# Batch 0's second product: block means copied at once, two masks on GpSimd, one pair's scores in a single excursion

## The chip, the cores and the metric

The kernel runs on one core of a Trainium2 chip. A core has a matrix engine (TensorE, PE in the profile), a vector engine (VectorE, DVE), an activation engine (ScalarE, ACT), a general engine (GpSimd, POOL) and a queue engine that issues transfers (SyncE, SP); transfers run on 16 DMA engines that all of these share. Each engine works through its own instructions strictly in the order in which the program lists them, and waits for the others at semaphores. The time is device microseconds for one execution, and the median over several executions is compared.

## The reference

Attention over 4 batches, 8 heads, 768 positions and head size 64, in which each position sees the 31 positions around it and 24 blocks of 32 positions in summary; then an MLP on the result.

```python
k_sum = k.reshape(B, H, nb, block, D).max(axis=3)      # block 32, nb 24
v_sum = v.reshape(B, H, nb, block, D).mean(axis=3)
scores_l = scale * np.matmul(q, k.transpose(0, 1, 3, 2))
mask_l = np.abs(pos[:, None] - pos[None, :]) < window  # window 16
scores_s = scale * np.einsum('bhsd,bhnd->bhsn', q, k_sum) + np.log(block)
scores_all = np.concatenate([np.where(mask_l, scores_l, -1e9), scores_s], axis=-1)
a = softmax(scores_all)
attn = np.matmul(a, np.concatenate([v, v_sum], axis=2))
x = attn.transpose(0, 2, 1, 3).reshape(B * S, H * D)   # 3072 x 512
h = x @ w_in                                           # 512 x 2048
out = (h * sigmoid(beta * h)) @ w_out                  # 2048 x 512
```

## The kernel before, in words

**Batches are staggered.** While the MLP of batch b runs on TensorE, the attention of batch b + 1 is woven into it. Each MLP has two products. The first (`h_half`, `h_tile`; lines 471 and 479) makes 16 tiles of h from xT, the transposed attention result. `h_tile` begins tiles 0 and 1 with twelve matmuls on xT of pairs 0 to 2 and only then takes pair 3's. The second makes 6 output tiles of 128 rows; each tile is 16 matmuls of 128x512 cut into 4 "atoms" of 4 matmuls (`o_atom`, matmul on line 497), so there are 24 atoms, numbered 0 to 23. The tiles alternate between two PSUM banks `one[0]` and `one[1]`; `o_out` copies a full tile to SBUF (on ScalarE for the first three tiles of batch 0, on VectorE otherwise) and SyncE stores it.

**Order by hand.** `run(main, sides)` lists the atoms; every side step carries a position, and a step with position p is issued behind atom floor(p), steps of one gap in the order of their positions. So a step at 8.99 comes behind atom 8 and one at 9.0 behind atom 9. The scheduler is manual: the order written is the order on each engine.

**Attention of batch 1 inside the second product of batch 0.** Heads go in 4 pairs g = 0 to 3, queries in two halves u = 0, 1.

- `scores(b, g, u, bg)` (matmuls on line 306) makes 24 score matmuls for both halves of a pair, 12 for each half, in the PSUM tile `big[2]` for u = 0 and `big[1]` for u = 1; `weigh` (line 315) takes the exponential on ScalarE into an SBUF tile `e` of 128x768; `mask_e` (line 319) multiplies that tile in place by the band mask on VectorE. In `scores` the mask follows at once for pairs 0 to 2. For pair 3 it follows inside `av`, behind the normalisation of pair 0.
- `vm_all` (line 368) makes the block means of all four pairs with 28 matmuls into `big[0]`, and four small copies, alternately on VectorE and ScalarE (`VMC`), take them to `vm_sb`.
- `spread(gg)` (line 379) copies the means of pairs 2gg and 2gg + 1 on VectorE into rows 96 to 127 of the two value tiles, two copies into `vo` and then two into `ve`. Before that, `v_odd_dma(g)` (lines 335 and 336) has moved shifted rows of `ve` to `vo` through SyncE's queue, reading those same rows of `ve`; the copies into `ve` wait for that transfer.
- `av_mm` (line 394) multiplies `e` by `ve` and `vo`, 24 matmuls for a pair, into `big[0]`, `big[1]`, `big[2]`, `big[0]` for pairs 0 to 3; `norm` (lines 420 and 421) divides by the sums on VectorE; `x_dma` (line 446) transposes the result into xT by a transfer that ScalarE's queue issues.
- `kq_cast` (line 455), on GpSimd, casts the keys of batch 2 as they arrive (`kst` to `kn`); the transfers that read `kn` are issued from SyncE (line 459) in the following stage.

Behind atom 8 lie `vm_all`, `spread(0)` and the scores of pair 2, half 0; behind atom 9 the scores of pair 2, half 1; behind atom 11 the scores of pair 3, `av` of pair 0 with the two masks of pair 3, and `spread(1)`; behind atom 14 `av` of pairs 1, 2 and 3.

Of the kernel before, what the change touches and what calls it, by code (L numbers as in the profile page):

```python
# [11 lines left out]
def kernel(  # L12
# [10 lines left out]
    nc = tc.nc  # L23
# [12 lines left out]
    QT = 64  # L36
# [5 lines left out]
    G = H // 2  # L42
# [224 lines left out]
    def km_pe(g, ks):  # L267
        key_max_win(g)
        key_sums(ks, g)
# [8 lines left out]
    def q_tile(g, h, m):  # L278
        return qn[g][h * D:(h + 1) * D, m * QT:(m + 1) * QT]
# [21 lines left out]
    def scores(b, g, u, bg):  # L301
        s = big[bg]
        for j in range(HT):
            m = u * HT + j
            for h in range(2):
                nc.tensor.matmul(s[:, h, j * QT:(j + 1) * QT], kw[g][h * D:(h + 1) * D, m, :], q_tile(g, h, m),  # L306
                                 start=True, stop=True)
        weigh(b, g, u, s)
        if g < G - 1:
            mask_e(b, g, u)  # L310

    def weigh(b, g, u, s):
        e = ep.tile([P, 2, HS], bf16, name="e", tag="e")
        et[(b, g, u)] = e
        return nc.scalar.activation(out=e[:], in_=s[:, :, 0:HS], func=ACTF.Exp, bias=bias[:, 0:1], scale=scale)  # L315

    def mask_e(b, g, u):
        e = et[(b, g, u)]
        nc.vector.tensor_mul(out=e.rearrange("p h (m q) -> p h m q", q=QT), in0=e.rearrange("p h (m q) -> p h m q", q=QT),  # L319
                             in1=mask[:, None, u * HT:(u + 1) * HT, :].to_broadcast([P, 2, HT, QT]))  # L320


# [11 lines left out]
    def v_odd_dma(g):  # L334
        nc.sync.dma_start(out=vo[0:QT, g, :, :], in_=ve[QT:P, g, :, :])
        nc.sync.dma_start(out=vo[QT:NK, g, 0:JV - 1, :], in_=ve[0:2 * W, g, 1:JV, :])
# [27 lines left out]
    def vm_all(t, cps):  # L364
        M = P - NK
        for j in range(J6 + 1):
            for g in range(G):
                nc.tensor.matmul(t[g * M:(g + 1) * M, 0, 0:2 * D], A[:, j],  # L368
                                 strided(ve[:, g, j, 0:1], [[J6 * VW, 2], [1, D]]),
                                 start=(j == 0), stop=(j == J6))  # L370
        for g in range(G):
            cps[g](vm_sb[NK:P, :, g], t[g * M:(g + 1) * M, 0, 0:2 * D].rearrange("p (h d) -> p h d", h=2))

    def spread(gg):
        r = slice(NK, P)
        s = slice(2 * gg, 2 * gg + 2)
        for tt in (vo, ve):
            for h in range(2):
                nc.vector.tensor_copy(out=tt[r, s, h * J6:(h + 1) * J6, 0:D],  # L379
                                      in_=vm_sb[r, h, s, None, :].to_broadcast([P - NK, 2, J6, D]))  # L380
# [5 lines left out]
    def av_mm(b, g, u, t):  # L386
        tv = t[:, 0:AVW].rearrange("p (j h e) -> p j h e", j=3, h=2)
        e = et[(b, g, u)]
        for j in range(3):
            J = 3 * u + j  # L390
            for h in range(2):
                for par in range(2):
                    lo = (2 * j + par) * QT
                    nc.tensor.matmul(tv[par * QT:(par + 1) * QT, j, h], e[:, h, lo:lo + QT],  # L394
                                     (vo if par else ve)[:, g, h * J6 + J, 0:D + 1], start=True, stop=True)
# [16 lines left out]
    def norm(b, g, t, us):  # L412
        t = t[:, 0:len(us)]
        n = len(us)
        if us[0] == 0:
            xn[(b, g)] = xp.tile([P, J6, 2, D], bf16, name="xn", tag="xn")
        x = xn[(b, g)]
        tv = t[:, :, 0:AVW].rearrange("p k (a e) -> p k a e", e=D + 1)
        r = xp.tile([P, n, 6], f32, name="r", tag="r")
        nc.vector.reciprocal(out=r[:], in_=tv[:, :, :, D])  # L420
        nc.vector.tensor_mul(out=x[:, 3 * us[0]:3 * us[0] + 3 * n].rearrange("p (k j) h d -> p k (j h) d", k=n),  # L421
                             in0=tv[:, :, :, 0:D], in1=r[:, :, :, None].to_broadcast([P, n, 6, D]))
# [188 lines left out]
    s = []  # L611
    wo = []

    def scale4(p, eng=None):
        for n in range(4 * p, 4 * p + 4):
            scale_w_out(n, eng)
# [18 lines left out]
    for g in (2, 3):  # L635
        s.append((g + .5, lambda g=g: mask_e(0, g, 1)))
# [6 lines left out]
    s = [(6, lambda: scale4(1)), (12, lambda: scale4(2)), (.5, clear_kw)]  # L643
# [11 lines left out]
    def scores_at(b, s, pos):  # L655
        for g in range(G):
            for u in range(2):
                s.append((pos[g] + .01 * u, lambda g=g, u=u: scores(b, g, u, (2, 1)[u])))
        s.append((pos[-1] + .02, silu_table))

    def av_at(b, s, pos, bufs):
        for g in range(G):
            def av(g=g):
                for u in range(2):
                    av_mm(b, g, u, big[bufs[g]][:, u])
                norm(b, g, big[bufs[g]], [0, 1])
                if g == 0:
                    for u in range(2):
                        mask_e(b, G - 1, u)
            s.append((pos[g], av))  # L670
# [9 lines left out]
    s = [(.05, exp_table), (.15, lambda: scale4(3)), (.7, lambda: km_pe(2, nc.gpsimd)), (2.9, lambda: km_pe(3, nc.gpsimd))]  # L680
    main = [lambda ms=ms, a=a: o_atom(0, ms, a) for ms in range(J6) for a in range(4)]
    for g in range(G):
        s.append(((2.5, 2.6, 2.7, 4.04)[g], lambda g=g: qt_pe(1, g, (0, 2, 1, 0)[g], dve_cp if g % 2 else act_cp)))
        s.append((3.3 + .1 * g, lambda g=g: v_cast(nc.gpsimd, g)))
        s.append((3.35 + .1 * g, lambda g=g: v_odd_dma(g)))
    scores_at(1, s, [4.05, 6.05, 8.99, 11.05])
    s.append((8.98, lambda: vm_all(big[0], VMC)))
    s.append((8.985, lambda: spread(0)))
    s.append((11.15, lambda: spread(1)))
    av_at(1, s, [11.1, 14.1, 14.2, 14.3], [0, 1, 2, 0])  # L690
    for g in range(G):
        s.append(((11.2, 14.35, 14.4, 14.5)[g], lambda g=g: x_dma(1, g)))
# [4 lines left out]
    for b in range(1, B):  # L697
        n = b + 1
        s = []
# [19 lines left out]
        s = [((x[0] - 16) * 1.2, x[1]) for x in late]  # L719
# [50 lines left out]
```

## Time and profile before

| | |
|---|---|
| median of 3 runs | 217.34 us (217.16, 217.34, 221.29) |
| profiled execution | 219.12 us |
| its span, first to last instruction | 217.4 us |
| around the span | 1.7 us |
| mean granted TensorE clock | 0.997 |
| TensorE busy | 206.3 us, 95% of the span |
| second product of batch 0 | 49.0 to 78.1 us |

Times in a view are microseconds from the first instruction. A row of a timeline has the start, the length, the engine, the line, the operation, what is written and read, and how many instructions are merged in it; in square brackets stands how long the engine was idle before it and what ended that idle time. The chain of waits follows the work that ended last back from the end: each piece was released by the one above it. In the view of one line or tile, three numbers with strokes are the shortest, the median and the longest instruction in ns.

### The profile page before, as it was taken

Reading aid. Unit: us, or ns where it says so; the run is one execution under the profiler, and the core shown is the slowest. Engines: PE = TensorE matmul, PEld = TensorE weight load, DVE = VectorE, ACT = ScalarE, POOL = GpSimd, SP = SyncE. Lnnn points to the kernel's source line nnn. Section 1 sums busy time; section 2 is a strip of 40 time slices with the busy share of each in tenths; the row PEclk is TensorE's granted clock in tenths of the full one; section 3 lists DMA queues with packets and bytes.
Section 4 is the critical chain, followed back from the end, with each engine's and each line's share of the span. In section 5 each row is a group of like instructions: output and inputs, shape, how many; then the busy total and the mean of one; then the engine's idle time right before and its main releaser. Section 6 shows DMA issues by size and latency. Waiting matters only on the chain.

```text
span 217.4 us, 5306 instructions
## 1 busy us (share of the span) xinstructions
PE 206.3 (95%) x2223; PEld 120.1 (55%) x2223; DVE 100.7 (46%) x235; ACT 107.6 (49%) x143; POOL 53.5 (25%) x88
## 2 busy tenths in 40 slices
PE   7779999999997999999999969999999999999993
PEld 7667666665454456664545436664555456654452
DVE  5576756697579611430799112521797200002121
ACT  2468586777773027667580037777570067750000
POOL 7928980010704200246103300246000000000000
PEclk9999999999999999999999999999999999999998
DMA  6999999999859939999669999999527410001212
GB/s 118 196 225 169 192 155 206 207 210 205 197 137 191 302 118 235 221 200 162 130 182 231 212 245 227 197 167 184 117 101 170 119 51 0 0 3 48 96 48 96
DMA packets 85271, 34.09 MB, mean 157 GB/s; under 512 B 73712, under 2 KB 82304, under 8 KB 85248
## 3 DMA queue, kind: packets, MB, share of 16 engines
q1 hardware_dynamic: 68192, 24.05, 54.5%
q0 software_dynamic: 7424, 7.34, 21.2%
q10 hardware_dynamic: 9632, 2.37, 7.2%
q8 instruction: 17, 0.28, 0.6%
q14 instruction: 6, 0.05, 0.1%
HBM read 27.37 MB, written 6.29 MB: 155 GB/s over the span
## 4 chain that ended last, share of the span: by engine, by line
PE 85%; DMA 7%; DVE 4%; issue 1%; POOL 1%; POOLq 0%; DVEq 0%
PE one L497 36%; PE big L479 28%; PE big L465 5%; DMA xT<-xn 4%; PE one L471 3%; DMA qrow<-in_q_dram 3%; PE big L306 3%; PE big L394 2%; PE big L255 2%; PE big L471 2%; DVE qn L242 1%; PE big L293 1%; PE big L285 1%; DVE xn L421 1%; PE big L368 1%
## 5 line engine op out<-in xcount | busy, mean ns | idle before, releaser
L497 PE MATMUL one<-w_out_sb,h_sb 128*128 128x512 bf16 (+1 forms) x400 | 86.5, 371 | 0.0
L492 ACT ACTIVATE h_sb<-big,beta_sb 128x768 bf16<-128x768 f32 x48 | 42.7, 900 | 55.5 <-PE big L479 55.5
L479 PE MATMUL big<-xT,w_in_sb 128*128 128x384 bf16 x384 | 63.1, 326 | 1.8 <-DMA xT<-xn 1.8
L497 PEld LDWEIGHTS <-h_sb 128*128 128x128 bf16 x400 | 37.7, 98 | 40.7 <-issue 0.2
L479 PEld LDWEIGHTS <-w_in_sb 128*128 128x128 bf16 x384 | 37.6, 98 | 27.1 <-issue 2.0
L242 DVE COPY o_sb<-one 128x512 f32<-128x512 f32 x20 | 13.8, 688 | 48.9 <-PE one L497 44.6
L315 ACT ACTIVATE e<-big,bias 128x768 bf16<-128x768 f32 x32 | 27.1, 898 | 7.9 <-PE big L306 4.9
L319 DVE TENSOR_TENSOR e<-e,mask 128x768 bf16<-128x768 bf16 x26 | 15.8, 631 | 18.0 <-ACT e L315 17.9
L236 POOL COPY kw<-km 128x288 bf16<-128x288 bf16 x12 | 5.2, 431 | 60.3 <-DVE km L232 38.7
L242 DVE COPY kw<-kT 128x1152 bf16<-128x1152 bf16 x8 | 3.8, 474 | 24.0 <-DMA kT<-kn 24.0
L324 POOL CAST ve<-vst 128x832 bf16<-128x832 f32 x15 | 13.3, 909 | 4.9 <-DMA vst<-in_v_dram 3.1
L455 POOL CAST kn<-kst 128x768 bf16<-128x768 f32 x8 | 6.9, 867 | 26.6 <-DMA kst<-in_k_dram 26.6
L421 DVE TENSOR_TENSOR xn<-big,r 128x768 bf16<-128x768 f32 (+1 forms) x14 | 12.6, 900 | 0.5
L232 DVE TENSOR_REDUCE km<-kT 128x24 bf16<-128x768 bf16 x12 | 11.2, 944 | 2.3 <-ACT kT L239 2.3
L465 PE MATMUL big<-xT,w_in_sb 128*128 128x384 bf16 x64 | 11.4, 326 | 0.0
L609 ACT ACTIVATE h_sb<-big,beta_sb 128x384 bf16<-128x384 f32 x16 | 8.1, 579 | 2.7 <-PE big L465 2.7
L471 PEld LDWEIGHTS <-w_in_sb 128*128 128x128 bf16 x64 | 6.1, 98 | 4.0
L394 PEld LDWEIGHTS <-e 128*64 128x64 bf16 x336 | 6.3, 111 | 3.4 <-issue 3.1
L471 PE MATMUL one<-xT,w_in_sb 128*128 128x384 bf16 x44 | 8.1, 326 | 0.0
L465 PEld LDWEIGHTS <-w_in_sb 128*128 128x128 bf16 x64 | 5.9, 98 | 3.5
L306 PEld LDWEIGHTS <-kw 64*128 64x128 bf16 x288 | 4.9, 95 | 4.8 <-issue 3.0
L394 PE MATMUL big<-ve,e 128*64 128x65 bf16 x150 | 6.4, 196 | 1.3 <-DVE ve L379 1.3
(121 smaller groups left out, 184.0 us busy)
## 6 DMA issues: line engine op xcount, KB each, us to landing
out_dram<-o_sb SPq DMA_DIRECT2D x23, 256.0 KB, 2.5
vst<-in_v_dram SPq DMA_DIRECT2D x13, 336.0 KB, 4.7
kst<-in_k_dram SPq DMA_DIRECT2D x8, 384.0 KB, 5.9
qst<-in_q_dram SPq DMA_DIRECT2D x8, 384.0 KB, 4.3
w_in_sb<-in_moe_w_in_dram POOLq DMA_DIRECT2D x4, 512.0 KB, 6.1
w_out_sb<-in_moe_w_out_dram POOLq DMA_DIRECT2D x4, 512.0 KB, 13.7
vo<-ve SPq DMA_DIRECT2D x12, 107.2 KB, 2.3
vst<-in_v_dram SPq DMA_DIRECT2D x3, 416.0 KB, 6.7
```

The source lines that it names most:

```text
L242: nc.vector.tensor_copy(out=o, in_=i)
L306: nc.tensor.matmul(s[:, h, j * QT:(j + 1) * QT], kw[g][h * D:(h + 1) * D, m, :], q_tile(g, h, m), start=True, stop=True)
L315: return nc.scalar.activation(out=e[:], in_=s[:, :, 0:HS], func=ACTF.Exp, bias=bias[:, 0:1], scale=scale)
L319: nc.vector.tensor_mul(out=e.rearrange("p h (m q) -> p h m q", q=QT), in0=e.rearrange("p h (m q) -> p h m q", q=QT), in1=mask[:, None, u * ...
L324: eng.tensor_copy(out=ve[:, g, lo:hi, 0:D], in_=vst[g][:, lo:hi])
L394: nc.tensor.matmul(tv[par * QT:(par + 1) * QT, j, h], e[:, h, lo:lo + QT], (vo if par else ve)[:, g, h * J6 + J, 0:D + 1], start=True, sto ...
L421: nc.vector.tensor_mul(out=x[:, 3 * us[0]:3 * us[0] + 3 * n].rearrange("p (k j) h d -> p k (j h) d", k=n), in0=tv[:, :, :, 0:D], in1=r[:, ...
L465: nc.tensor.matmul(t[:, 0:HS], w_in_sb[:, ki, i * P:(i + 1) * P], xT[:, ki, 0:HS], start=(ki == 0), stop=(ki == k1 - 1))
L471: nc.tensor.matmul(t[:, 0:HS], w_in_sb[:, ki, i * P:(i + 1) * P], xT[:, ki, lo:lo + HS], start=(ki == 0), stop=(ki == k1 - 1))
L479: nc.tensor.matmul(t[:, kk, 0:HS], w_in_sb[:, ki, i * P:(i + 1) * P], xT[:, ki, kk * HS:(kk + 1) * HS], start=(ki == 0), stop=(ki == k1 - 1))
L492: nc.scalar.activation(out=h_sb[:, i, :].rearrange("p (k m) -> p k m", k=2), in_=t[:, :, 0:HS], func=ACTF.Silu, scale=beta_sb[:, i:i + 1])
L497: nc.tensor.matmul(t[:, 0:hi - lo], h_sb[:, n, ms * P:(ms + 1) * P], w_out_sb[:, n, lo:hi], start=(n == 0), stop=(n == k2 - 1))
```

## The change

Four edits, all for batch 1's attention inside the second product of batch 0. The later batches keep their order and their engines.

1. `spread(1)` moves from behind atom 11 (position 11.15) to behind atom 8 (8.982), right behind `spread(0)` and ahead of pair 2's scores.
2. The two masks of pair 3 are issued in `scores`, right behind the exponentials, and on GpSimd instead of VectorE; `av` of pair 0 issues them no longer.
3. Pair 2's scores move from 8.99 and 9.00 to 8.985 and 8.995, so that both halves come behind atom 8 with no atom between them.
4. `spread(0)` moves from 8.985 to 8.981, which keeps it ahead of pair 2's scores.

```diff
@@ scores(b, g, u, bg)
         weigh(b, g, u, s)
-        if g < G - 1:
+        if g < G - 1 or b == 1:
             mask_e(b, g, u)
@@ mask_e(b, g, u)
-        nc.vector.tensor_mul(out=e.rearrange(
+        (nc.gpsimd if (b, g) == (1, G - 1) else nc.vector).tensor_mul(out=e.rearrange(
...
@@ av_at(b, s, pos, bufs)
                 norm(b, g, big[bufs[g]], [0, 1])
-                if g == 0:
+                if g == 0 and b > 1:
                     for u in range(2):
                         mask_e(b, G - 1, u)
@@ second product of batch 0
-    scores_at(1, s, [4.05, 6.05, 8.99, 11.05])
+    scores_at(1, s, [4.05, 6.05, 8.985, 11.05])
     s.append((8.98, lambda: vm_all(big[0], VMC)))
-    s.append((8.985, lambda: spread(0)))
-    s.append((11.15, lambda: spread(1)))
+    s.append((8.981, lambda: spread(0)))
+    s.append((8.982, lambda: spread(1)))
     av_at(1, s, [11.1, 14.1, 14.2, 14.3], [0, 1, 2, 0])
```

The resulting order on the engines: on VectorE, the four copies of `spread(1)` now follow those of `spread(0)`, then the two masks of pair 2, then the four normalisations. On GpSimd, the two masks of pair 3 stand between the last cast of values (line 324) and the first cast of batch 2's keys (line 455). ScalarE and SyncE keep their order.

More of the change, by code (lines that the diff above doesn't have):

```diff
@@ L318, in mask_e @@
         e = et[(b, g, u)]
-        nc.vector.tensor_mul(out=e.rearrange("p h (m q) -> p h m q", q=QT), in0=e.rearrange("p h (m q) -> p h m q", q=QT),
+        (nc.gpsimd if (b, g) == (1, G - 1) else nc.vector).tensor_mul(out=e.rearrange("p h (m q) -> p h m q", q=QT), in0=e.rearrange("p h (m q) -> p h m q", q=QT),
                              in1=mask[:, None, u * HT:(u + 1) * HT, :].to_broadcast([P, 2, HT, QT]))
```

## The prediction

> **What bounds the kernel now.** I read the page first, then the chain of waits in order of time, then the timeline of each engine over the second product of batch 0.
>
> ```profile
> span 217.4 us, 5306 instructions
> PE 206.3 (95%) x2223; PEld 120.1 (55%) x2223; DVE 100.7 (46%) x235; ACT 107.6 (49%) x143; POOL 53.5 (25%) x88
> ```
>
> TensorE is busy 95% of the span, so a change elsewhere pays only where TensorE stands still or spends time on switching. The chain of waits (start, length, what) shows this stage and, from 111 us, the same stage of the next batch:
>
> ```profile
> 60.29 0.28 PE big L306 x12
> 60.58 0.97 PE one L497 x4
> 61.55 0.28 PE big L306 x12
> 61.83 1.83 PE one L497 x8
> 63.66 0.46 PE big L306 x24
> 64.12 0.55 PE big L394 x24
> ...
> 66.29 1.18 DVE e L319
> ...
> 67.48 0.63 DVE vo L379 x2
> 68.11 1.18 DVE ve L379 x2
> 69.29 0.04 issue
> 69.33 0.92 PE big L394 x44
> 70.25 7.88 PE one L497 x36
> 78.13 20.80 PE big L479 x128
> ...
> 111.58 2.70 PE one L497 x12
> 114.27 1.26 PE big L394 x72
> ...
> 120.01 7.98 DMA xT<-xn
> ```
>
> Between 64 and 69 us the chain leaves TensorE: normalisation, masks of pair 3 and the copies of `spread(1)` run on VectorE, and the last two of those copies release the product with the values. TensorE's own timeline shows the hole:
>
> ```profile
> 64.55 2.76 PE L497 MATMUL one<-w_out_sb,h_sb 128*128 128x512 bf16 x12
> 67.24 0.22 PE L394 MATMUL big<-ve,e 128*64 128x65 bf16 x1
> 69.06 0.19 PE L394 MATMUL big<-ve,e 128*64 128x65 bf16 x1 [1.25 <-DVE ve L379]
> 70.19 7.94 PE L497 MATMUL one<-w_out_sb,h_sb 128*128 128x512 bf16 x36
> ```
>
> Pairs 1 to 3 take from 67.24 to 70.19, 2.95 us. In the next batch the same 72 matmuls take 1.26. So 1.69 us are lost here, and no removal of this wait can give more.
>
> **Pair 2 in one excursion.** Two visits of 12 score matmuls, with 4 and then 8 output matmuls, take 0.28 + 0.97 + 0.28 + 1.83 = 3.36 us (60.29 to 63.66). In one visit 24 score matmuls take 0.46 (63.66) and the 12 output matmuls behind them 2.70 (111.58): 3.16. Gain 0.2, so everything behind it on TensorE comes 0.2 earlier: pair 3's scores at 63.46, atoms 12 to 14 ending at 67.04 instead of 67.24. The second half needs `big[1]`, which the exponential of pair 1 left long before, and ScalarE's order does not change:
>
> ```profile
> 61.56 1.69 ACT L315 ACTIVATE e<-big,bias 128x768 bf16<-128x768 f32 x2
> 63.70 0.58 ACT L239 COPY o_sb<-one 128x512 f32<-128x512 f32 x1 [0.45 <-PE one L497]
> 64.18 1.70 ACT L315 ACTIVATE e<-big,bias 128x768 bf16<-128x768 f32 x2
> ```
>
> **The block means earlier.** VectorE gets four copies ahead of pair 2's masks:
>
> ```profile
> 61.82 0.62 DVE L379 COPY ve<-vm_sb 32x768 bf16<-32x768 bf16 x2
> 62.49 0.56 DVE L319 TENSOR_TENSOR e<-e,mask 128x768 bf16<-128x768 bf16 x1
> ...
> L335 SPq DMA_DIRECT2D vo<-ve x1: 483/483/483, 61.0 to 61.0; - x1
> DMA to landing us min/median/max: 2.2/2.2/2.2
> ```
>
> `spread(0)` ends at 62.44. The two `vo` copies of `spread(1)` take 0.63 (row 67.48) to 63.07. The two `ve` copies must wait for pair 3's shift transfer, issued at 61.0 and landed 2.2 later, at 63.2; so this wait costs 0.15, and queued behind it are pair 2's masks and the normalisation of pair 0. The copies end at 63.85. Pair 2's exponentials end at 62.4 and 63.25 (row 61.56), so its masks, 0.54 apart, run to 64.95, and the normalisation of pair 0 (0.23 + 0.96) ends at about 66.15, where it ended at 65.91. Who waits for these: pair 2's product at 67.04 + 0.42 = 67.46 for the masks, 2.5 us of slack; pair 3's product at 67.88 for `big[0]`, which the normalisation empties, 1.7 us of slack; and pair 0's transposing transfer, 0.2 us later. Nothing on TensorE's path. That is the first edit's price: nothing, with these slacks as cover.
>
> **The masks on GpSimd.** This is what is late next. The exponentials of pair 3 start 0.2 earlier with the atom that precedes them, at 63.98, and end at 64.83 and 65.68. GpSimd has been idle since its last value cast, so it starts about 64.88. TensorE wants half 0 of pair 3 at 67.88 and half 1 at 68.09. Two masks of t each release half 1 at 64.88 + 2t; with 0.05 for the signal (0.04 in the row at 69.29) and 0.21 for the last 12 matmuls, TensorE leaves at 65.14 + 2t, but not before 67.04 + 1.26 = 68.30.
>
> No GpSimd instruction with two tensor inputs is in the trace, so t is bounded by neighbours:
>
> ```profile
> 66.03 1.03 POOL L455 CAST kn<-kst 128x768 bf16<-128x768 f32 x1 [6.66 <-DMA kst<-in_k_dram]
> 67.85 0.95 POOL L455 CAST kn<-kst 128x768 bf16<-128x768 f32 x1 [0.79 <-DMA kst<-in_k_dram]
> 70.36 0.83 POOL L455 CAST kn<-kst 128x768 bf16<-128x768 f32 x1 [1.56 <-DMA kst<-in_k_dram]
> L319 DVE TENSOR_TENSOR e<-e,mask x2: 547/790/1033, 58.8 to 59.7; 128x768 bf16<-128x768 bf16 x2
> L319 DVE TENSOR_TENSOR e<-e,mask x2: 548/862/1177, 65.8 to 66.3; 128x768 bf16<-128x768 bf16 x2
> ```
>
> One input of 768 elements costs 0.83 undisturbed (70.36) and 1.03 beside VectorE (66.03). Below: t = 0.83, if the second input is free. Above: 2 x 1.03 = 2.06, if the inputs are read one behind the other and disturbed. I take 2 x 0.83 = 1.66, since a cast already moves an element in about the time that reading one takes, and VectorE has little of the disturbing kind left there. With it TensorE leaves at 68.46 instead of 70.19: 1.73 gained, of 1.89 (0.2 + 1.69) at most; at 2.06, 69.26 and 0.93. The Trainium skill, "GPSIMD Engine Reference", section 4.1 "Engine selection", speaks against the edit: it gives elementwise products to VectorE, and section 3.1 has 4497 ns for 2048 elements of a two-input add. An estimate by that figure is 1.69 us for 768, and the sum would be 0.06 less; no run so far shows the operation.
>
> The second cost is a collision. Alone a mask on VectorE takes 0.55; the one begun at 66.29 took 1.18 and ended at 67.47, 0.41 behind the cast that had begun at 66.03 and ended at 67.06. So it stood until GpSimd was done. Pair 2's second mask starts at 64.4, GpSimd at 64.88: VectorE is first, and GpSimd may start 0.1 late, which I charge. If it is the other way round, the mask stands until 64.88 + 1.66 = 66.54, ends at 66.95, and the normalisation of pair 0 at 68.15, 0.27 behind TensorE's need of `big[0]`: TensorE leaves at 68.15 + 0.05 + 0.42 = 68.62, 0.16 worse. The Trainium skill, "SBUF — State Buffer", says of the port pair that the two engines share that it is "an exclusive lock, not a bandwidth split"; the 1.18 against 0.55 agrees.
>
> Behind the masks on GpSimd stand the key casts: the first moves from 66.03 to about 68.3. Their readers are transfers issued at 81.48:
>
> ```profile
> 81.48 2.54 SPq L459 DMA_TRANSPOSE kT<-kn  x1
> ```
>
> That is cover of some 10 us. Moving the masks off VectorE also removes two instructions (64.95 to 67.47 in the chain is mostly theirs), so the normalisations of pairs 1 to 3 run at 67.5, 68.7 and 69.8 without a queue.
>
> **What is late after that.** TensorE reaches the next product 1.63 earlier, at 76.5, and wants xT of pairs 0 to 2 there, and of pair 3 twelve matmuls on (20.80/128 x 12 = 1.95), at 78.45.
>
> ```profile
> L446 ACTq DMA_TRANSPOSE xT<-xn x2: 1252/1274/1296, 71.9 to 73.3; - x2
> DMA to landing us min/median/max: 3.6/3.6/3.6
> DMA to landing us min/median/max: 3.6/4.0/7.3
> ```
>
> Before, pairs 2 and 3 were issued at 71.9 and 73.3 and landed 3.6 later, at 75.5 and 76.9, against needs at 78.13 and 80.08. After, they are issued at about 70.0 and 71.3 and land by 73.6 to 75.6. The slack stays above 2 us.
>
> **Sum.** 0.2 from the single excursion, 1.69 from the hole, less 0.16 for half 1 of pair 3 and 0.1 for the collision: 1.63 us. The profiled execution, 219.12 with its span of 217.4, would lose that from its span: 215.8. The median of the runs, 217.34, is below that execution; the same 1.63 off it gives 215.7.
>
> **Rivals.**
>
> *GpSimd is slower than two reads.* Break-even is 65.14 + 2t = 70.19, t = 2.5 us. At four times the single read, 3.3 us, TensorE leaves at 71.74, 1.55 later than before: 218.9. For it: GpSimd has no such row here. Against: its one-input rows lie at 0.83 to 1.03. Chance 0.17, from 217.3 upward.
>
> *A first-use price on GpSimd.* If the first product there has to fetch its code, the whole stage waits. Against it: the first copy of its kind is as quick as the rest.
>
> ```profile
> 8.79 0.52 POOL L331 COPY vo<-ve 64x384 bf16<-64x384 bf16 x1
> 18.48 0.50 POOL L331 COPY vo<-ve 64x384 bf16<-64x384 bf16 x1
> ```
>
> It loses from 1.63 us up, and 2% from 4.35 + 1.63 = 6 us up; priced at that edge, 217.34 + 4.35 = 221.7. The same page of the Trainium skill, section 2.1, puts a first call into a freshly loaded kernel library at about 6 us; nothing here shows such a load. Chance 0.05.
>
> *The gain meets a late transfer.* With 7.3 us to landing, as the slowest had it (beside the key loads), instead of 3.6, pair 2's transfer would land at 70.0 + 7.3 = 77.3, 0.8 behind the need: 216.5. Chance 0.12. Further on, the next stage ends in a transfer of 7.98 us (120.01) that TensorE waits for. If that end were fixed by transfers that do not move with TensorE, all would be lost: 217.3. Against: the loads of that stage stand on SyncE's queue behind the output stores, which move along. Chance 0.06.
>
> **How the numbers follow.** Forecast 215.7 with 0.60, its own range 215.3 to 216.4 (t from 0.83 to 2.06, and 0.1 to 0.2 of spread between runs). The range to 217.9 takes in both transfer cases and the near edge of the slow mask: 0.8 of the chance; its low end, 215.2, is 217.34 less 1.89 less 0.2. About 2%, 4.35 us here, is what a measurement of this kernel can tell from no change. The holes are too small for a gain of 4.35; a loss of that size needs the first-use price or masks of 4.7 us each: 0.06.
>
> **What would show it.** In the profile after: a single visit of 24 score matmuls near 60.3; `spread(1)` ending near 63.9; two rows of GpSimd on line 319 of about 1.66 us each, the first near 64.9; pairs 1 to 3 on TensorE in about 1.4 us from 67.0, with at most a wait of 0.2 on GpSimd; the next product starting near 76.5 without a wait on xT. Rows of GpSimd over 2.5 us, or a wait on xT at 76.5, make it wrong.

## The result and the profile after

| | before | changed |
|---|---|---|
| median of 20 runs each | 218.32 us (216.97 to 221.29) | 217.12 us (215.01 to 220.72) |
| ratio | | 0.994, 95% interval 0.9915 to 0.9966 |
| profiled execution, its span | 219.12, 217.4 us | 219.29, 217.6 us |

The change is faster by 0.6%: 1.3 us by the ratio, 0.7 to 1.9 by its interval. The ratio counts only executions within 1.5% of the fastest of the same kernel; the medians count all. The forecast was 215.7 us, which is 1.6 us under the 217.34 us of the three runs that were known, but 2.6 us under the 218.32 us that the same kernel has over 20 runs.

The page of the changed kernel, with the row of the granted TensorE clock in 40 slices of 5.4 us:

```profile
span 217.6 us, 5307 instructions
PEclk9958999999999999999999999999999999999999
```

The profiled execution had a low clock from about 11 to 22 us, long ahead of the change, so the two spans cannot be set against each other, and I compare stages: from the first output matmul (line 497) to the first matmul of the next product (line 479). Over all sets of runs, the executions that the ratio counts and whose mean granted clock was 0.997 or more have means of 217.6 us before (51 runs) and 216.6 changed (20 runs), 1.0 us apart.

The chain of waits of the changed kernel through the stage (start, length, what):

```profile
62.28 0.51 PE big L368 x28
62.79 0.46 PE big L306 x24
63.24 2.71 PE one L497 x12
...
65.98 0.49 ACT o_sb L239
66.46 0.91 ACT e L315
...
67.45 3.25 POOL e L319 x2
...
70.75 0.38 PE big L394 x12
71.13 7.88 PE one L497 x36
79.00 20.80 PE big L479 x128
```

One visit of 24 score matmuls, then 12 output matmuls, as drawn up. The chain now leaves TensorE for ScalarE's exponential and GpSimd's two masks instead of VectorE's queue. The timelines of VectorE and GpSimd beside it:

```profile
65.41 0.62 DVE L379 COPY ve<-vm_sb 32x768 bf16<-32x768 bf16 x2
66.06 1.03 DVE L319 TENSOR_TENSOR e<-e,mask 128x768 bf16<-128x768 bf16 x2
67.45 3.24 POOL L319 TENSOR_TENSOR e<-e,mask 128x768 bf16<-128x768 bf16 x2 [6.04 <-ACT e L315]
70.64 1.60 POOL L455 CAST kn<-kst 128x768 bf16<-128x768 f32 x2
```

The masks of pair 2 are over at 67.09, before GpSimd starts; GpSimd's two take 3.24, 1.64 each by the instruction; the key casts wait behind them and nobody waits for those.

The lengths of the parts in us, read from the starts of these matmuls in every profile. "Hole" is the time that TensorE stood still behind another engine ahead of the products with the values (line 394), from its timeline. "Over 20.80" is what the next first product took over its 20.80 us, mostly the wait on xT near 125 us.

| profile | ahead of the stage | hole | stage | over 20.80 |
|---|---|---|---|---|
| before | 49.0 | 1.25 | 28.95 | 1.97 |
| before, c1 | 49.2 | 1.19 | 28.88 | 3.89 |
| before, d1 | 50.6 | 1.30 | 28.99 | 0.48 |
| before, d2 | 48.6 | 0.53 | 28.22 | 0.00 |
| n1, before without key loads | 52.0 | 1.25 | 28.94 | 0.00 |
| n3, the same again | 48.9 | 1.23 | 28.92 | 0.00 |
| changed | 51.5 | under 0.1 | 27.32 | 1.27 |
| changed, c0 | 49.5 | under 0.1 | 27.32 | 0.35 |
| changed, d1 | 49.1 | under 0.1 | 27.32 | 1.29 |
| changed, d2 | 49.0 | under 0.1 | 27.32 | 1.57 |
| n2, changed without key loads | 49.0 | under 0.1 | 27.31 | 0.00 |
| e1, masks on VectorE | 49.5 | under 0.1 | 27.12 | 0.42 |
| e8, the same again | 48.9 | under 0.1 | 27.26 | 0.76 |
| e2, means early only | 49.0 | under 0.1 | 27.26 | 1.39 |
| e3, one excursion only | 48.9 | 1.19 | 28.67 | 0.67 |
| e4, masks on GpSimd only | 51.4 | 1.88 and 0.68 | 31.77 | 0.41 |
| e5, second mask twice | 49.2 | 1.78 | 29.03 | 0.48 |
| e6, changed, later key loads | 49.1 | under 0.1 | 27.33 | 0.31 |
| e7, e1 with later key loads | 49.2 | under 0.1 | 27.05 | 1.73 |
| e9, keys late in the kernel before | 51.0 | under 0.1 | 27.69 | 1.36 |

The stage went from 28.95 to 27.32, 1.63 us: the forecast's sum to the hundredth. It is the same in all four profiles of the changed kernel. What is not the same is the stage of the kernel before (28.22 in one of its profiles) and the wait on xT at the end of the next stage, which both kernels have. It was the first of these rows of waits in the first profile of the kernel before, and the second in that of the changed kernel:

```profile
PE big L479 <- DMA xT<-xn: 1.8, 1, 1.8
...
PE big L479 <- DMA xT<-xn: 1.1, 1, 1.1
```

### The profile page after: what moved, and what is told of

It is laid out like the page before. It is cut to its first block, busy times and chain, and to the rows that moved or that the text cites. A ratio compares the mean times of both kernels' runs of the same rounds, so it can differ in the third digit from the quotient of the medians.

```text
span 217.6 us, 5307 instructions
## 1 busy us (share of the span) xinstructions
PE 208.4 (96%) x2223; PEld 122.1 (56%) x2223; DVE 99.1 (46%) x233; ACT 107.8 (50%) x143; POOL 56.9 (26%) x90
## 4 chain that ended last, share of the span: by engine, by line
PE 85%; DMA 7%; POOL 3%; DVE 2%; issue 1%; ACT 1%; POOLq 0%; DVEq 0%
PE one L497 35%; PE big L479 28%; PE big L465 5%; DMA xT<-xn 4%; PE one L471 3%; DMA qrow<-in_q_dram 3%; PE big L255 2%; PE big L306 2%; PE big L394 2%; PE big L471 2%; POOL e L319 1%; PE big L293 1%; PE big L368 1%; POOL krow L85 1%; PE big L285 1%
## 5 line engine op out<-in xcount | busy, mean ns | idle before, releaser
L319 DVE TENSOR_TENSOR e<-e,mask 128x768 bf16<-128x768 bf16 x24 | 13.7, 592 | 18.2 <-ACT e L315 18.0
L473 ACT ACTIVATE h_sb<-one,beta_sb 128x384 bf16<-128x384 f32 x11 | 6.4, 582 | 1.5 <-PE one L471 1.0
```

Of the source, the lines that this page charges most:

```text
L319: (nc.gpsimd if (b, g) == (1, G - 1) else nc.vector).tensor_mul(out=e.rearrange("p h (m q) -> p h m q", q=QT), in0=e.rearrange("p h (m q) ...
```

## The experiments

**The changed kernel again, and the edits one by one.** c0, e1, e2 and e3 were run against the same runs of the kernel before.

c0 is the changed kernel itself:

> The changed kernel once more, as the control of this set. Theory (the stage gives 1.63 us and keeps it): about 1.6 us under the kernel before run beside it, ratio 0.9925. Rival (some of the gain is met by the transposing transfer that TensorE waits for at the end of the next stage): the stage is still 1.6 us shorter, but the ratio lies at 0.995 to 0.998 and the wait on xT near 128 us is longer than in the kernel before.

Ratio 0.9962, interval 0.993 to 0.9994: 0.1 to 1.5 us, again less than the stage's 1.63. The ratio lies where the rival put it, but not for the rival's reason: the wait at the end of the next stage was shorter here (0.35 against 1.97), not longer.

e1 keeps the masks of pair 3 on VectorE (shown against the changed kernel):

```diff
-        if g < G - 1 or b == 1:
+        if g < G - 1:
...
-        (nc.gpsimd if (b, g) == (1, G - 1) else nc.vector).tensor_mul(
+        nc.vector.tensor_mul(
...
-                if g == 0 and b > 1:
+                if g == 0:
```

> All of the change but the GpSimd edit: the two masks of pair 3 stay on VectorE behind the normalisation of pair 0. Theory (the hole came from the late copies of the block means, and GpSimd's 1.62 us masks leave a wait of 0.2 to 0.3 us): the masks end by 68.0 on the clock of the kernel before, TensorE does not wait, the stage is 1.8 to 1.9 us shorter than before and 0.2 shorter than in the changed kernel; ratio 0.991 to 0.992. Rival (VectorE's queue was the trouble, so the masks must leave it): the masks, which also meet the key casts on GpSimd, end after 68.6, TensorE waits for them by 0.5 us or more, and the kernel is slower than the changed one.

Ratio 0.9871 (0.9813 to 0.9928, six runs); e8, the same kernel again:

> The variant with the masks of pair 3 on VectorE once more, since its first set had few runs. By its stage (1.83 us shorter than before, with no wait left in it) 216.0 to 216.2 where the kernel before has 217.9, ratio 0.991 to 0.993. The 0.987 of its first set would need 2.8 us, more than the stage lost; if it comes again, something behind the stage has gained too.

Ratio 0.9936 (0.9903 to 0.9968), 1.4 us, where its stage is 1.69 shorter; the 0.987 did not come again. In e1 VectorE's masks run beside a key cast, as the timelines of GpSimd and VectorE show:

```profile
66.82 1.20 POOL L455 CAST kn<-kst 128x768 bf16<-128x768 f32 x1 [7.48 <-DMA kst<-in_k_dram]
66.78 1.64 DVE L319 TENSOR_TENSOR e<-e,mask 128x768 bf16<-128x768 bf16 x2
```

They take 1.64 instead of 1.03, and still the chain of waits has TensorE do its 72 matmuls in 1.33, against 1.26 undisturbed:

```profile
67.53 1.33 PE big L394 x72
```

So the GpSimd edit was not needed. Without it the stage is 0.06 to 0.20 shorter. That lead over the changed kernel is too small for the timing to settle.

e2 moves only `spread(1)` (and `spread(0)` to stay ahead of it) in the kernel before:

```diff
-    s.append((8.985, lambda: spread(0)))
-    s.append((11.15, lambda: spread(1)))
+    s.append((8.981, lambda: spread(0)))
+    s.append((8.982, lambda: spread(1)))
```

> Only the copies of the block means of pairs 2 and 3 move ahead; masks on VectorE as before, pair 2's scores in two visits. Theory: it alone removes the hole, 1.6 to 1.7 us, ratio 0.992. Rival (each edit gives a share): under 1 us.

Stage 27.26, so this one edit alone shortens it by 1.69, as much as the whole change does; ratio 0.9929 (0.9887 to 0.9972). Its chain shows pairs 1 to 3 without a stop:

```profile
67.29 1.26 PE big L394 x72
```

e3 moves only pair 2's scores (and `spread(0)` to stay ahead of them) in the kernel before:

```diff
-    scores_at(1, s, [4.05, 6.05, 8.99, 11.05])
+    scores_at(1, s, [4.05, 6.05, 8.985, 11.05])
...
-    s.append((8.985, lambda: spread(0)))
+    s.append((8.981, lambda: spread(0)))
```

> Only pair 2's scores are put into one visit. Theory: 0.2 us less between the first scores of pair 2 and the scores of pair 3 (3.16 us instead of 3.36), and nothing of it reaches the end, since TensorE then waits 0.2 longer for VectorE or arrives 0.2 earlier with VectorE's work: 0 to 0.2 us, ratio 0.999 to 1.000. Rival (switching costs more than the trace shows): 0.5 us or more.

Stage 28.67, 0.28 less; ratio 0.9985 (0.9949 to 1.0021), which the timing cannot tell from nothing. Against the five profiles of the kernel before and of n1 and n3 that have the full hole (28.88 to 28.99) it is 0.21 to 0.32 less, so all of the 0.21 by which pair 0's product starts earlier reaches the end of the stage; I had expected 0 to 0.2.

**What GpSimd does to VectorE.** e4 is the GpSimd edit alone in the kernel before, with the copies of block means still behind the normalisation of pair 0.

```diff
-        nc.vector.tensor_mul(
+        (nc.gpsimd if (b, g) == (1, G - 1) else nc.vector).tensor_mul(
...
-        if g < G - 1:
+        if g < G - 1 or b == 1:
             mask_e(b, g, u)
...
-                if g == 0:
+                if g == 0 and b > 1:
```

> Only the masks of pair 3 go to GpSimd; the four late copies of block means stay behind the normalisation of pair 0 on VectorE, where they now run beside GpSimd's masks. Theory (a VectorE instruction of this kind stands until GpSimd's instruction is done): the first copy takes about 0.7 us or more instead of 0.35, some copy ends about 0.3 to 0.4 us behind a mask of GpSimd, and TensorE leaves the stage 0 to 1.2 us earlier than before. Rival (the engines do not hinder each other): the copies take 0.35 us each, 66.0 to 67.2, and TensorE leaves 1.4 us earlier, held by the second mask alone.

The four copies, in the view of their line (shortest, median, longest ns):

```profile
L379 DVE COPY vo<-vm_sb x2: 1092/1441/1790, 68.3 to 69.3; 32x768 bf16<-32x768 bf16 x2
L379 DVE COPY ve<-vm_sb x2: 973/974/975, 71.0 to 71.9; 32x768 bf16<-32x768 bf16 x2
```

GpSimd's timeline beside them:

```profile
67.55 3.35 POOL L319 TENSOR_TENSOR e<-e,mask 128x768 bf16<-128x768 bf16 x2 [6.26 <-ACT e L315]
70.85 2.75 POOL L455 CAST kn<-kst 128x768 bf16<-128x768 f32 x3
```

A copy of 0.35 us took 1.09, 1.79, 0.97 and 0.97: each stood behind one instruction of GpSimd, two masks and two casts, and the engines took turns. The direction of the theory holds and its size does not: I had put the stage at 0 to 1.2 us shorter, and it is 2.8 longer, since every copy was hit, the last two by the casts behind the masks. The chain of waits shows a second loss, and the windows the clock beside it:

```profile
72.97 1.33 PE big L394 x45
74.30 9.04 PE one L497 x36
```

```profile
70.00:80.00 10.00, 7.44 (x82) 3.82 (x77) 6.98 (x11) 0.00 (x0) 4.43 (x5) 0.83 1.05 208
```

In that window (columns after the length: busy time of PE, PEld, DVE, ACT, POOL, then the granted clock) TensorE stood still for 2.56 us, the clock was 0.83, and the 36 matmuls that take 7.88 elsewhere took 9.04.

**Are GpSimd's masks the end of the stage?** e5 is the changed kernel with half 1's mask multiplied in once more.

```diff
             mask_e(b, g, u)
+        if (b, g, u) == (1, G - 1, 1):
+            mask_e(b, g, u)
```

> The changed kernel with the mask of pair 3, half 1, multiplied in twice on GpSimd (0 and 1, so the values stay). Theory (GpSimd's masks end last in this stage): TensorE leaves 1.6 us later than in the changed kernel, the whole length of one mask, and the stage is as long as in the kernel before. Rival (the masks are hidden): less than 1 us later.

The chain of waits of this run:

```profile
65.16 3.24 POOL e L321 x2
68.40 0.07 issue
68.47 1.64 POOL e L321
...
70.15 0.38 PE big L396 x12
```

Stage 29.03 against 27.32: 1.71 us for a mask of 1.64. They do end last, with no slack.

**The wait on xT.** e6 and e7 load batch 3's keys later, in the changed kernel and in e1:

```diff
-                s.append((7, lambda n=n: load_keys(n + 1)))
+                s.append((15.5, lambda n=n: load_keys(n + 1)))
```

> The changed kernel with the key loads of batch 3 issued behind atom 15 instead of atom 7 of batch 1's second product, so that they follow the transposing transfers of batch 2. Theory (those loads slow the transposing transfers, 6 to 8 us to landing instead of 3.6 to 4): xT lands before TensorE needs it, the wait of 1.1 to 1.8 us near 128 us goes, and the kernel is 1 to 1.8 us faster than the changed one, ratio 0.985 to 0.988 against the kernel before. Rival (the transfers are slow for another reason, or the later keys are missed in the next stage): no gain, or a new wait of VectorE and TensorE for the keys between 130 and 150 us.

> The same later key loads, with the masks of pair 3 on VectorE. If both readings hold, it is 0.2 us faster than the run before it and the fastest of all, ratio 0.984 to 0.987; if the loads are the only thing, it equals the run before it.

Ratios 1.0118 (1.0079 to 1.0157) and 1.0093 (1.0058 to 1.0129): slower. In e6 TensorE has no wait on xT, but the keys are missed one stage on; its chain:

```profile
123.54 6.48 DMA kst<-in_k_dram
...
133.56 6.04 DMA kT<-kn
...
149.42 3.56 DMA vst<-in_v_dram
```

The third second product took 29.28 us instead of 25.35. In e7 the loads, issued from 118.0, met the last transposing transfer, issued at 118.1, and the wait was 1.57 all the same; its third second product took 27.23.

n1 and n2 leave those loads out, in the kernel before and in the changed one:

```diff
-                s.append((7, lambda n=n: load_keys(n + 1)))
+                stg.update({("k", n + 1, g): stg[("k", n, g)] for g in range(G)})
```

> The kernel before without the key loads of batch 3: batch 3 uses the keys of batch 2 that lie in the buffers, so its output is another. It shows what those four loads of 384 KB cost through the transposing transfers beside them. Theory (they are why xT lands 6 to 8 us after its issue at the end of the next stage): the wait on xT near 128 us is gone, and the kernel is 0.5 to 1.5 us faster than before. Rival (the wait has another cause): the wait stays at 0.5 us or more.

> The changed kernel without the same loads. Theory (the stage's 1.63 us were met in part, in some executions, by the wait on xT): without that wait this run is 1.6 us, 0.75%, faster than the previous one, more than the 1.0 to 1.3 us measured with the loads in. Rival (the stage is worth less in time than its trace shows, for a cause that has nothing to do with xT): the difference stays near 1 us. Second rival (the measured difference was only spread): the two differences agree within their intervals, and the profiles show no wait that grew.

> The kernel before without the key loads of batch 3, profiled again (batch 3 uses the keys of batch 2). If the missing 0.4 us are collisions that come in some executions only, the stage is 28.2 us here; if they are ahead of the stage, that part is 48.5 us or less; if neither, the stage is 28.9 and the part ahead 49.0, and they stay open.

The next first product takes 20.80 in all three profiles: no wait. (The second product ahead of it takes 25.58 to 25.78 instead of 25.35.) So those loads are what delays xT in the others. The ratios are 0.9945 (0.9913 to 0.9977) and 0.9932 (0.9892 to 0.9973). The two are only 0.3 us apart, but half of n2's executions had a clock under 0.997; at 0.997 or more the means are 216.6 (8 runs) and 215.5 (6 runs), 1.1 us apart. That is hardly more than with the loads in, so the wait on xT is not where the rest of the stage's gain goes. n3 has the full hole, no wait on xT and an ordinary part ahead of the stage (48.9), and its 217.16 is above seven of those eight runs of n1. Those seven must be shorter somewhere; that it is in the hole is not shown.

**The kernel before as its own control, and more profiles.**

> The kernel before as its own control: ratio 1.000 within an interval of 0.003 to 0.004, which is what the other ratios have to be read against; and one more profile of its wait on xT near 128 us, which is 1.8 us in the first. If that wait depends on the execution and not on the kernel, it differs from 1.8 by 0.5 us or more.

Ratio 1.0006 (0.997 to 1.0043). The wait on xT was 2.05 us, and the product behind it lost 1.8 us more at a low clock (last section). Then two more profiles of each kernel:

> The kernel before, profiled for the lengths of its parts. Stage 28.9 to 29.0 us. If the part ahead of the stage is shorter for this kernel than for the changed one, it lies at 48.5 to 49.0; if the wait on xT takes the rest, it is under 0.5 us here.

> The changed kernel, profiled likewise. Stage 27.3 us. If the part ahead of the stage is where 0.4 us go, it lies at 49.1 to 49.5; if the wait on xT is, it is over 0.5 us here; if it is only spread, both parts overlap with those of the kernel before.

> The kernel before again: stage 28.9 to 29.0 us, the part ahead and the wait on xT within 0.3 us of the first profile if the program sets them, further apart if the execution does.

> The changed kernel again: stage 27.3 us, and the same reading of the part ahead and of the wait on xT.

The table above has them. The part ahead and the wait on xT vary by execution in both kernels. What I had not listed as possible came up in d2 of the kernel before: the stage itself was 0.73 us shorter. (That it had no wait on xT is no gain in full: its next second product took 26.13 us instead of 25.35.) Its timelines of GpSimd, VectorE and TensorE in the hole:

```profile
66.17 0.95 POOL L455 CAST kn<-kst 128x768 bf16<-128x768 f32 x1 [7.20 <-DMA kst<-in_k_dram]
65.42 1.02 DVE L319 TENSOR_TENSOR e<-e,mask 128x768 bf16<-128x768 bf16 x2
66.45 1.16 DVE L379 COPY vo<-vm_sb 32x768 bf16<-32x768 bf16 x2
67.53 0.62 DVE L379 COPY ve<-vm_sb 32x768 bf16<-32x768 bf16 x2
67.93 0.19 PE L394 MATMUL big<-ve,e 128*64 128x65 bf16 x1 [0.53 <-DVE ve L379]
```

Here the first key cast starts after both masks have begun, so it hits only one copy (1.16 for two instead of 0.63), and the second cast, at 67.94, comes when the last copy has begun. In the first profile one mask (1.18) and one copy of `ve` were hit, as its timeline of VectorE shows:

```profile
65.83 1.64 DVE L319 TENSOR_TENSOR e<-e,mask 128x768 bf16<-128x768 bf16 x2
67.48 0.63 DVE L379 COPY vo<-vm_sb 32x768 bf16<-32x768 bf16 x2
68.03 1.25 DVE L379 COPY ve<-vm_sb 32x768 bf16<-32x768 bf16 x2
```

In c1, d1 and n3 it was one mask and one copy of `vo`, and in n1 the same two as in the first profile.

**The collisions taken out.** e9 is the kernel before with batch 2's key loads issued behind atom 11:

```diff
-    s.append((6.5, lambda: load_keys(2)))
+    s.append((11.5, lambda: load_keys(2)))
```

> The kernel before, with the key loads of batch 2 issued behind atom 11 instead of atom 6 of batch 0's second product; none of the four edits. Theory (1.25 us of the hole are two VectorE instructions that stand behind key casts on GpSimd): no key cast lies in the hole, the two masks take 1.0 us and the two pairs of copies 0.6 each, the hole closes 1.2 us earlier and the stage is 27.7 us instead of 28.9. Rival (the length of the queue on VectorE makes the hole, not the collisions): the stage stays at 28.5 us or more.

```profile
67.77 1.02 DVE L319 TENSOR_TENSOR e<-e,mask 128x768 bf16<-128x768 bf16 x2
68.81 0.63 DVE L379 COPY vo<-vm_sb 32x768 bf16<-32x768 bf16 x2
69.36 0.62 DVE L379 COPY ve<-vm_sb 32x768 bf16<-32x768 bf16 x2
71.10 0.83 POOL L455 CAST kn<-kst 128x768 bf16<-128x768 f32 x1 [10.24 <-DMA kst<-in_k_dram]
```

No cast lies in the hole, every VectorE instruction has its undisturbed length, and the stage is 27.69, with none of the four edits. So 1.26 of the 1.69 us that the prediction calls the hole were collisions with key casts: 0.63 for the mask (1.18 less 0.55) and 0.63 for the copies (1.25 less 0.62). The remaining 0.43 I put down to the length of VectorE's queue, through which the chain of waits still runs in e9. This is one execution, with a low clock ahead of the stage; whether the kernel as a whole gets faster by it was not timed.

## Why the prediction was right, and where it was wrong

- **Single excursion, 0.2 us:** right. Pair 1's product with the values starts 18.01 us behind the first output matmul in the changed kernel and 18.22 before, 0.21 earlier.
- **Block means early, at no cost:** right, and worth the whole gain (e2). The wait for the shift transfer was absent in the changed kernel and 0.49 in e1, hidden both times.
- **The masks on GpSimd, t = 1.66 from two single reads:** 1.64 measured. e5 shows that the masks end last. The cost of 0.16 for that came out larger: pairs 1 to 3 are through at 19.54 us behind the first output matmul, where 18.01 and 1.26 without a stop make 19.27.
- **Collision with pair 2's masks, 0.1 us:** it did not come about; VectorE was through 0.36 us before GpSimd began.
- **xT at 76.5 us in time:** right in the outcome; no profile of the changed kernel has a wait there. The slack of over 2 us was not there: pair 2's transfer landed 5.2 to 5.4 us after its issue in the changed kernel's four profiles, not 3.6, and 0.6 to 0.8 us ahead of the product.
- **Sum, 1.63 us:** 28.95 to 27.32 is 1.63. That it fits to the hundredth is luck: the wait on the masks was 0.1 larger and the collision's 0.1 absent, and the other profiles of the kernel before give 1.56, 1.67 and 0.90.
- **Rivals:** a slow GpSimd and a first-use price are refuted by rows of 1.64 us from the first one on. That the gain would meet a late transfer further on is refuted as the cause of the shortfall by n1 and n2; the wait there exists, in both kernels, and comes from the key loads.

**The step that failed** is the last sentence of the sum: "the same 1.63 off" the median of the runs, 217.34, "gives 215.7". The measured median is 1.4 us above that, and two terms of the step were off. The larger is the base: three runs gave 217.34, twenty gave 218.32, and one of the three had already shown 221.29. Off the larger base the sum gives 216.7, and 217.12 was measured. That 217.12 lies inside the range of 215.2 to 217.9 is luck too: its upper part was there for late transfers and slow masks, and neither came.

The smaller is the gain: 1.63 was taken for the time of every execution, and 1.0 to 1.3 us came. The sum treated the hole as a property of the program. The rows that it quoted itself, a mask of 1.18 against 0.55 and in the chain two `ve` copies of 1.18 behind two `vo` copies of 0.63, said that most of the hole was collisions with casts, whose time depends on when keys land. The collision was priced for the new order and not for the old one, from which it was to be taken away. Where it is smaller, as in d2, the change has less to remove: 0.9 us in the stage instead of 1.63.

How often the smaller hole comes is not known. It came in one of the six profiles of the kernel before and of the same without key loads (n1, n3), and at that rate it takes 0.1 us off the mean gain, where 0.3 to 0.6 us are missing between trace and time. The first set's interval, 0.7 to 1.9 us, still holds 1.63; that of c0, 0.1 to 1.5, does not. So the shortfall of the gain is explained in kind at most and not in size, and its cause stays open.

## What to carry to other kernels

Where an instruction in a stall is longer than its twins, ask what made it longer before counting the stall: that part can belong to a neighbour, vary from run to run, and be removed at the neighbour too, as in e9. Work moved to GpSimd was paid for twice here, by its own length (e5) and by VectorE's block-mean copies that stood behind it (e4); the order alone, with the masks left where they were, did as well (e1, e2, e8). Take the base of a forecast from as many runs as there are, and let the range hold the spread of the base.

## What was not expected of the hardware

With GpSimd running four instructions in a row and VectorE four copies (e4), each copy waited for one GpSimd instruction, and copies of 0.35 us took 0.97 to 1.79: the engines alternated, and VectorE's queue ran at GpSimd's pace. The Trainium skill, "SBUF — State Buffer", section "Who interferes with whom", has the one that comes later stand until the other is done; these rows agree, and add that a queue of such instructions on both sides interleaves one by one. VectorE's normalisation, which reads PSUM and one SBUF operand, was not touched: 0.96 us beside GpSimd's masks as without them.

And where TensorE stood for 2.56 us in e4, in two pieces of 1.88 and 0.68, its granted clock was 0.83 over that window of 10 us, while the hole of the kernel before, 1.25 us, left it at 1.00, and so did the 1.78 us of e5. In c1 a low clock followed the single wait of 2.05 us on xT; the row of the clock on its page dips in the slice from 126 to 132 us:

```profile
PEclk9999999999999999999999979999999999999999
```

The first product that begins there took 24.69 us instead of 20.80, so the wait and the low clock behind it cost 3.89 together.
